# First layer of two small items with both halves of x in one matmul, and second-layer weights read as loaded

## The chip, the core and the metric

The kernel runs on one core of one Trainium2 chip. The metric is the time of one execution in microseconds (us), the median of several runs. The engines go by the names of the profile: PE is TensorE (with PEld for its weight loads), DVE is VectorE, ACT is ScalarE, POOL is GpSimd, SP is SyncE, whose queue issues most of the loads from memory.

## The reference

First a windowed attention over 8 sequences of 576 tokens and 8 heads; its output, 4608 tokens of 512 numbers, goes to a mixture of experts. Tokens with a positive skip score are sent to the best of 8 experts, a two-layer network, and its result, weighted with the gate, is added.

```python
skip_score = x @ w_skip
do_compute = skip_score > 0
xc = x[do_compute]
logits = xc @ w_gate
e_idx = np.argmax(logits, axis=1)
gate_w = softmax(logits)[np.arange(len(xc)), e_idx]
for e in range(8):
    mask = e_idx == e
    h = np.maximum(xc[mask] @ w1[e], 0.0)        # 512 -> 1024
    y[mask] = gate_w[mask, None] * (h @ w2[e])   # 1024 -> 512
out[do_compute] = xc + y
```

## The kernel before

The attention fills the first 162 us of the profiled execution; the change doesn't touch it. Towards its end the tokens are counted and listed for the experts, and the experts' work begins.

**Items and steps.** The experts are ranked by their number of tokens, and each rank has a fixed capacity. An item is a block of tokens of one expert: 256, 256, 144 (the rest of the second expert), 368, 336, 288, 256, 240, 160 and 112 (the rest of the first). Each item has four steps, one for each quarter (256 hidden units) of its expert. In step k the generator `expert_chunks` emits the first layer of step k (`up`) and the second layer of step k - 2 (`down`).

**Two parts of every operand.** Products are made in three matmuls: each operand is split into a rounded high part and a low rest, and `mm3` adds high by high, high by low and low by high in PSUM. For x this gives the tiles xh and xl, for the weights whi and wlo, for the hidden layer hh and hl.

**First layer.** For items of more than 128 tokens `up` makes two halves (f = 0, 1) of 128 hidden units each. In each it runs over four chunks c of 128 inputs, with three matmuls per chunk: the weights are the stationary operand, x of all n tokens the moving one, the sum stands in the PSUM tile p1 (tag "t", two buffers, in turn). Then ScalarE makes hh = relu(p1), rounded, and VectorE makes hl = max(p1, 0) - hh. Where the last 128-token tile of an item has 32 tokens or fewer (the items of 144, 288 and 160; the code calls them small), ScalarE also makes hp, a plain copy of relu(p1) for these last tokens.

**Second layer.** `down` multiplies tile by tile with `mm3`; for the last tile of a small item `down_small` multiplies hp with plain fp32 weights instead, four narrow matmuls side by side. These weights are loaded a second time for that purpose by `load_plain` into the tiles wr (256 KB a time, four buffers).

**Weights.** Each expert has eight pieces of 128 x 1024 numbers (512 KB): four of the first layer (w = 0) and four of the second (w = 1). SP's queue loads a piece into one of six raw tiles (`weight_dma`), ScalarE copies it rounded to whi (`weight_hi`), VectorE subtracts for wlo (`weight_lo`). whi and wlo stand in a ring of nine slots, each free again after the last use of its piece. `weights_to` is called before each chunk of the generator; it loads ahead by up to six pieces beyond the last one split and splits one more piece per chunk while the ring has room.

**x of the next item** is fetched by an indirect load (`gather_x`) and transposed on TensorE into the PSUM tile px (tag "g", one buffer); ScalarE copies xh and VectorE subtracts for xl (`split_x`). This happens within the steps of the item before, at the points (quarter, half) in `SPLITS`, after the `yield` of that half, so that the next weight split is emitted first.

**Order.** The order of the instructions on each engine is that of the program, with no planner: each engine takes its own in turn and waits at the first that isn't ready.

Of the kernel before, what the change touches and what calls it, by code (L numbers as in the profile page):

```python
# [8 lines left out]
F32 = mybir.dt.float32  # L9
# [4 lines left out]
ALU = mybir.AluOpType  # L14
# [51 lines left out]
OOB = 1 << 20  # L66
NWR = 4
XN = max(n for _, n, _ in ITEMS)
# [75 lines left out]
def window_attention_moe(ctx: ExitStack, tc, a, out):  # L144
# [667 lines left out]
    ring, used = [], {}  # L812
    raws = [early.tile([P, 1024], F32, name=f"raw{i}") for i in range(NRAW)]

    def ring_slots(pool, n):
# [12 lines left out]
    def weight_dma(n):  # L828
        e, qi, w = pieces[n]
        if e not in wrow:  # L830
            r = e % E
            ix = perm[0:1, r : r + 1] if r < 2 else tables["order"][0:1, r : r + 1]
            wrow[e] = nc.values_load(ix, engines=[SP], min_val=0, max_val=(E - 1) * NQ * P)
        nc.sync.dma_start(
            raws[n % NRAW], a["wq"][bass.ds(wrow[e] + qi * P, P), w * 1024 : w * 1024 + 1024]
        )
# [5 lines left out]
    def weight_hi(n):  # L842
        nc.scalar.copy(ring[n % RING][0], raws[n % NRAW])  # L843

    def weight_lo(n, by):
        hi, lo = ring[n % RING]
        by.tensor_tensor(lo, raws[n % NRAW], hi.bitcast(F32), op=ALU.subtract)  # L847

# [4 lines left out]
    def weights_to(n):  # L853
        n = min(n, len(pieces), ptr["free"] + len(ring))
        while ptr["split"] < n:
            while ptr["dma"] < min(len(pieces), ptr["split"] + NRAW):
                if not can_load(ptr["dma"]):
                    break
                weight_dma(ptr["dma"])
                ptr["dma"] += 1  # L860
            if ptr["dma"] == ptr["split"]:
                break
            weight_split(ptr["split"])
            ptr["split"] += 1
        while ptr["dma"] < min(len(pieces), ptr["split"] + NRAW) and can_load(ptr["dma"]):
            weight_dma(ptr["dma"])
            ptr["dma"] += 1
# [3 lines left out]
    def can_load(n):  # L871
        return pieces[n][0] % E < 2 or "order" in tables
# [42 lines left out]
    class Item:  # L915
        def __init__(self, n, e=None):
# [3 lines left out]
            self.small = self.nt > 1 and self.rows[-1] <= 32  # L920
            self.hh, self.hl, self.hp, self.wr = {}, {}, {}, {}

# [8 lines left out]

        def split(self, xh, xl, j, px=None):
            xh, xl = xh[:, :, : self.n], xl[:, :, : self.n]
            self.xc = [(xh[:, c], xl[:, c]) for c in range(NDC)]
            return split_x(self.xg[j], xh, xl, j, px)

        def split_both(self, xh, xl, pxs):
            self.xc = [(xh[c // 2][:, c % 2], xl[c // 2][:, c % 2]) for c in range(NDC)]
            split_both(self.xg, xh, xl, pxs)
# [4 lines left out]
    def up(it, qi, wh, wl):  # L944
# [6 lines left out]
        if nt > 1:  # L951
            for f in range(2):
                p1 = psum.tile([P, n], F32, name="p1", tag="t", bufs=2, padded_shape=[P, 512])
                for c in range(NDC):
                    w = slice(c * FQ + f * P, c * FQ + f * P + P)
                    mm3(p1, wh[:, w], wl[:, w], *it.xc[c], c == 0, c == NDC - 1)
                nc.scalar.activation(hh[:, f], p1, AF.Relu)  # L957
                if it.small:
# [5 lines left out]
        else:  # L964
# [11 lines left out]
            nc.vector.tensor_tensor(hl, pt[:, :, :n], hh.bitcast(F32), op=ALU.subtract)  # L976

    def load_plain(it, h):
        if h < 2 * NQ:
            it.wr[h] = wr = hpool["y"].tile([P, D], F32, name="wr", bufs=NWR)  # L980
            c = 1024 + h % 2 * D
            nc.sync.dma_start(wr, a["wq"][bass.ds(wrow[it.e] + h // 2 * P, P), c : c + D])

# [31 lines left out]
    def down_small(it, qi, y, m):  # L1015

        for f in range(2):
            h = 2 * qi + f
            for z in range(4):
                nc.tensor.matmul(  # L1020
                    y[32 * z : 32 * z + m, 0:P],
                    it.hp[qi][:, f, :m],
                    it.wr[h][:, z * P : (z + 1) * P],
                    start=h == 0,
                    stop=h == 2 * NQ - 1,
                    skip_group_check=True,
                )
            load_plain(it, h + NWR)

# [45 lines left out]
    def expert_chunks():  # L1075
        for k in range(len(steps) + 2):
            rising = ()
            if k < len(steps):
                i, qi = steps[k]
                if its[i].small and qi == 1:  # L1080
                    for h in range(NWR):
                        load_plain(its[i], h)
                rising = up(its[i], qi, *piece(k, 0))
                for f, c in enumerate(rising):
                    yield k, c
                    if its[i].nt == 1:
                        break
                    if i + 1 < len(its):
                        pts = ((3, 0), (3, 2)) if i + 1 == 2 else SPLITS[its[i + 1].nt]
                        if (qi, f) in pts:  # L1090
                            its[i + 1].split(*xhl[1 + i % 2], pts.index((qi, f)))()
            if k >= 2:
# [27 lines left out]
    with tc.manual_schedule():  # L1120
# [136 lines left out]
        tables["lists"] = mr.tile([P, E, LT], I32, name="les")  # L1257
        xhl += [tuple(mr.tile([P, NDC, XN], F32R, name=f"x{h}{s}") for h in "hl") for s in "12"]
        ring_slots(mr, RING - len(ring))
        xfree.extend(xgs[4:])  # L1260

# [204 lines left out]
```

## Time and profile before

| | us |
|---|---|
| median of 3 runs | 421.97 (420.9 to 422.24) |
| the profiled execution, its own time | 418.07 |
| its span, first to last instruction | 416.3 |
| TensorE busy | 398.2 (96% of the span) |
| VectorE busy | 291.6 (70%) |
| ScalarE busy | 219.4 (53%) |

The profile is of one execution. The 144-token item takes its steps from 210.8 us of the span on, the 160-token item from 372.3 us on. Matmuls are pipelined: a row's duration includes the way through the array, so what a matmul costs in a stream is read from the distance between starts. In the list of instructions in order of time, a bracket at the end of a line gives the idle time of the engine before it and what ended it.

### The profile page before, as it was taken

Reading aid. Unit: us, or ns where it says so; the run is one execution under the profiler, and the core shown is the slowest. Engines: PE = TensorE matmul, PEld = TensorE weight load, DVE = VectorE, ACT = ScalarE, POOL = GpSimd, SP = SyncE. Lnnn points to the kernel's source line nnn. Section 1 sums busy time; section 2 is a strip of 40 time slices with the busy share of each in tenths; the row PEclk is TensorE's granted clock in tenths of the full one; section 3 lists DMA queues with packets and bytes.
Section 4 is the critical chain, followed back from the end, with each engine's and each line's share of the span. In section 5 each row is a group of like instructions: output and inputs, shape, how many; then the busy total and the mean of one; then the engine's idle time right before and its main releaser. Section 6 shows DMA issues by size and latency. Waiting matters only on the chain.

```text
span 416.3 us, 11734 instructions
## 1 busy us (share of the span) xinstructions
PE 398.2 (96%) x4687; PEld 334.5 (80%) x4687; DVE 291.6 (70%) x515; ACT 219.4 (53%) x389; POOL 157.6 (38%) x296
## 2 busy tenths in 40 slices
PE   8699999999999889899999999999999999999994
PEld 3587887878778678779988898898888889988873
DVE  3387899899799797999436679555556485656661
ACT  2477868767767695436224436234426355444540
POOL 1431168666958878557103115013016030100110
PEclk9999999999999999899999999999999999999999
DMA  8999999999995695636928937545388866667810
GB/s 296 406 326 375 408 368 382 410 386 310 366 413 195 204 362 173 196 128 219 311 82 254 324 117 258 183 161 205 117 250 291 264 206 202 221 203 244 265 55 23
DMA packets 38554, 105.73 MB, mean 254 GB/s; under 512 B 4864, under 2 KB 6272, under 8 KB 38496
## 3 DMA queue, kind: packets, MB, share of 16 engines
q1 hardware_dynamic: 34016, 93.51, 65.3%
q0 software_dynamic: 3200, 9.58, 6.5%
q10 hardware_dynamic: 1280, 1.85, 1.2%
q8 instruction: 38, 0.62, 0.6%
q14 instruction: 20, 0.16, 0.1%
HBM read 90.86 MB, written 14.39 MB: 253 GB/s over the span
## 4 chain that ended last, share of the span: by engine, by line
PE 68%; DMA 10%; issue 7%; DVE 7%; POOL 4%; ACT 2%; POOLq 0%; ACTq 0%; DVEq 0%
PE av L387 8%; PE p L911 7%; PE p L912 7%; PE p L913 7%; PE pt L284 6%; PE ps L251 5%; DMA out<-yo,les 5%; PE yv L911 3%; PE yw L911 3%; PE yw L912 3%; PE yw L913 3%; PE yv L912 3%; PE yv L913 3%; DMA q<-qT 2%; PE ps L237 2%
## 5 line engine op out<-in xcount | busy, mean ns | idle before, releaser
L847 DVE TENSOR_TENSOR wlo<-raw,whi 128x1024 fp32r<-128x1024 f32 x70 | 85.6, 1233 | 17.5 <-ACT whi L843 17.5
L957 ACT ACTIVATE hh<-p 128x256 fp32r<-128x256 f32 (+6 forms) x72 | 27.7, 384 | 127.3 <-PE p L913 123.0
L911 PE MATMUL p<-xh,whi 128*128 128x256 f32 (+6 forms) x288 | 85.9, 298 | 0.2 <-DVE hl L960 0.2
L912 PE MATMUL p<-xl,whi 128*128 128x256 f32 (+6 forms) x288 | 84.3, 293 | 0.8 <-DVE xl L892 0.8
L913 PE MATMUL p<-xh,wlo 128*128 128x256 f32 (+6 forms) x288 | 84.4, 293 | 0.6 <-DVE wlo L847 0.6
L843 ACT CAST whi<-raw 128x1024 fp32r<-128x1024 f32 x72 | 74.3, 1046 | 0.0
L1003 POOL DMA_INDIRECT out<-yo,les x18 | 17.6, 976 | 147.3 <-DVE yo L994 137.6
L960 DVE SCALAR_TENSOR_TENSOR hl<-p,hh 128x256 fp32r<-128x256 f32 (+6 forms) x72 | 30.1, 419 | 61.2 <-ACT hh L957 35.5
L911 PEld LDWEIGHTS p<-xh,whi 128*128 128x128 f32 x288 | 55.2, 192 | 3.7 <-issue 1.7
L912 PEld LDWEIGHTS p<-xl,whi 128*128 128x128 f32 x288 | 55.3, 192 | 2.1 <-DVE xl L892 1.1
L913 PEld LDWEIGHTS p<-xh,wlo 128*128 128x128 f32 x288 | 55.4, 192 | 0.8 <-DVE wlo L847 0.8
L276 ACT ACTIVATE s<-s 128x1024 f32<-128x1024 f32 x36 | 38.1, 1058 | 30.9 <-DVE s L271 30.8
L270 DVE TENSOR_REDUCE mx<-ps 128x8 f32<-128x1024 f32 x36 | 43.6, 1210 | 6.1 <-PE ps L251 6.1
L271 DVE TENSOR_TENSOR s<-ps,mx 128x1024 f32<-128x1024 f32 x36 | 44.1, 1225 | 4.6
L387 PEld LDWEIGHTS av<-vm,ptm 128*64 128x64 f32 x992 | 35.2, 138 | 12.2 <-issue 5.5
L387 PE MATMUL av<-vm,ptm 128*64 128x74 f32 x992 | 40.4, 233 | 3.4 <-POOL vm L356 1.4
L285 ACT COPY ptm<-pt 128x512 f32<-128x512 f32 x72 | 38.3, 581 | 5.9 <-PE pt L284 5.8
L284 PE MATMUL pt<-ident,s 128*128 128x128 f32 x288 | 39.9, 283 | 0.0
L251 PE MATMUL ps<-k,q 64*64 64x128 f32 x1024 | 33.6, 270 | 2.5 <-DMA q<-qT 2.5
L251 PEld LDWEIGHTS ps<-k,q 64*64 64x64 f32 x1024 | 30.0, 133 | 5.3 <-issue 3.1
L284 PEld LDWEIGHTS pt<-ident,s 128*128 128x128 f32 x288 | 31.6, 143 | 2.5 <-issue 0.3
L356 POOL COPY vm<-vm 64x1184 f32<-64x1184 f32 x16 | 18.6, 1166 | 34.9 <-ACT vm L355 29.2
(225 smaller groups left out, 699.9 us busy)
## 6 DMA issues: line engine op xcount, KB each, us to landing
raw<-wq SPq DMA_DIRECT2D x72, 512.0 KB, 4.7
vm<-vp SPq DMA_DIRECT2D x15, 592.0 KB, 9.1
vT<-vT SPq DMA_DIRECT2D x16, 512.0 KB, 8.3
out<-x SPq DMA_DIRECT2D x32, 256.0 KB, 7.3
q<-qT SPq DMA_DIRECT2D x14, 512.0 KB, 9.1
wr<-wq SPq DMA_DIRECT2D x24, 256.0 KB, 5.5
k<-kT SPq DMA_DIRECT2D x7, 640.0 KB, 8.6
k<-kT SPq DMA_DIRECT2D x7, 512.0 KB, 8.7
```

Source lines behind the costliest of these rows:

```text
L251: nc.tensor.matmul(ps[64 * hf : 64 * hf + 64, r, p], q[h, p], k[h, :, p], start=False, stop=p == 3, skip_group_check=True,)
L270: nc.vector.tensor_reduce(mx, flat, axis=AX.X, op=ALU.max)
L271: pace[0] = nc.vector.tensor_tensor(s, flat, mx.unsqueeze(2).to_broadcast([P, 8, P]), op=ALU.subtract)
L276: nc.scalar.activation(s, s, AF.Exp, scale=0.125)
L284: nc.tensor.transpose(pt[:, p], s[:, 4 * r + p], ident)
L285: nc.scalar.copy(ptm[:, 4 * r : 4 * r + 4], pt)
L387: nc.tensor.matmul(av[64 * hf : 64 * hf + 64, h // 4, (h % 4) * VW : (h % 4 + 1) * VW], ptm[:, (h % 2) * 4 + h // 2, 64 * hf : 64 * hf + 6 ...
L843: nc.scalar.copy(ring[n % RING][0], raws[n % NRAW])
L847: by.tensor_tensor(lo, raws[n % NRAW], hi.bitcast(F32), op=ALU.subtract)
L911: nc.tensor.matmul(o, lh, rh, start=first, stop=False, skip_group_check=parts)
L912: nc.tensor.matmul(o, lh, rl, start=False, stop=False, skip_group_check=parts)
L913: nc.tensor.matmul(o, ll, rh, start=False, stop=last, skip_group_check=parts)
```

## The change

- Items of more than 128 and up to 160 tokens (those of 144 and 160) keep xh and xl of a chunk side by side in one tile. In the first layer one matmul with whi moves both (2n columns), and one with wlo adds its product to the second half. VectorE adds the two halves of p1 with a reduce into a tile in SBUF (`rest`; the tile is hs for f = 0 and the finished table `found` for f = 1), makes hh from it with a max, and then hl. hp is made by ScalarE from `rest`.
- `down_small` reads its weights from the raw tile of the piece. `load_plain` and wr are gone. The raw tiles are handed out from a list (`idle`): a tile goes back after wlo is made, or, for the second-layer pieces of the three experts that have a small tile, after `down_small`. Two more raw tiles are added once the attention's memory is free, eight in all.
- The split of the next item's x stands before the `yield` of its half instead of behind it, so ahead of the next weight split. One of the splits, the second of the 144-token item's x, stays where it was.

```diff
@@ weights
+    idle, raw_of = list(raws), {}
+    plain = {e for _, n, e in ITEMS if P < n and 0 < n % P <= 32}
+    held_raw = lambda n: pieces[n][2] == 1 and pieces[n][0] in plain
...
+        raw_of[n] = idle.pop(0)
         nc.sync.dma_start(
-            raws[n % NRAW], a["wq"][bass.ds(wrow[e] + qi * P, P), w * 1024 : w * 1024 + 1024]
+            raw_of[n], a["wq"][bass.ds(wrow[e] + qi * P, P), w * 1024 : w * 1024 + 1024]
         )
...
-        by.tensor_tensor(lo, raws[n % NRAW], hi.bitcast(F32), op=ALU.subtract)
+        by.tensor_tensor(lo, raw_of[n], hi.bitcast(F32), op=ALU.subtract)
+        if not held_raw(n):
+            idle.append(raw_of.pop(n))
...
-            while ptr["dma"] < min(len(pieces), ptr["split"] + NRAW):
+            while ptr["dma"] < len(pieces) and idle:
@@ Item.split
-        def split(self, xh, xl, j, px=None):
+        def split(self, xh, xl, pair, j, px=None):
             xh, xl = xh[:, :, : self.n], xl[:, :, : self.n]
+            self.pairs = [pair[:, c, :, : self.n] for c in range(NDC)] if P < self.n <= PAIRED else None
@@ up
-                p1 = psum.tile([P, n], F32, name="p1", tag="t", bufs=2, padded_shape=[P, 512])
+                p1 = psum.tile([P, 2 * n if it.pairs else n], F32, name="p1", tag="t", bufs=2, padded_shape=[P, 512])
                 for c in range(NDC):
                     w = slice(c * FQ + f * P, c * FQ + f * P + P)
-                    mm3(p1, wh[:, w], wl[:, w], *it.xc[c], c == 0, c == NDC - 1)
-                nc.scalar.activation(hh[:, f], p1, AF.Relu)
+                    if it.pairs:
+                        nc.tensor.matmul(
+                            p1, wh[:, w], it.pairs[c], start=c == 0, stop=False, skip_group_check=True
+                        )
+                        nc.tensor.matmul(
+                            p1[:, n:], wl[:, w], it.xc[c][0],
+                            start=False, stop=c == NDC - 1, skip_group_check=True,
+                        )
+                    else:
+                        mm3(p1, wh[:, w], wl[:, w], *it.xc[c], c == 0, c == NDC - 1)
+                if it.pairs:
+                    room = found.rearrange("p v e j -> p (v e j)") if f else pool.tile([P, FQ], F32, name="hs")
+                    rest = room[:, :n]
+                    nc.vector.tensor_reduce(rest, p1.rearrange("p (z n) -> p n z", z=2), axis=AX.X, op=ALU.add)
+                    p1 = rest
+                    nc.vector.tensor_scalar(hh[:, f], p1, 0.0, None, op0=ALU.max)
+                else:
+                    nc.scalar.activation(hh[:, f], p1, AF.Relu)
                 if it.small:
                     nc.scalar.activation(hp[:, f, : it.rows[-1]], p1[:, n - it.rows[-1] :], AF.Relu)
@@ down_small
+        n = when[it.e, qi, 1]
...
-                    it.wr[h][:, z * P : (z + 1) * P],
+                    raw_of[n][:, f * D + z * P : f * D + (z + 1) * P],
...
-            load_plain(it, h + NWR)
+        idle.append(raw_of.pop(n))
@@ expert_chunks
-                if its[i].small and qi == 1:
-                    for h in range(NWR):
-                        load_plain(its[i], h)
                 rising = up(its[i], qi, *piece(k, 0))
                 for f, c in enumerate(rising):
+                    if i + 1 < len(its) and its[i].nt > 1:
+                        pts = ((3, 0), (3, 2)) if i + 1 == 2 else SPLITS[its[i + 1].nt]
+                        if (qi, f) in pts:
+                            its[i + 1].split(*xhl[1 + i % 2], pts.index((qi, f)))()
                     yield k, c
                     if its[i].nt == 1:
                         break
-                    if i + 1 < len(its):
-                        pts = ((3, 0), (3, 2)) if i + 1 == 2 else SPLITS[its[i + 1].nt]
-                        if (qi, f) in pts:
-                            its[i + 1].split(*xhl[1 + i % 2], pts.index((qi, f)))()
@@ once the attention's memory is free
+        for s in "12":
+            pair = mr.tile([P, NDC, 2, XN], F32R, name=f"xp{s}")
+            xhl.append((pair[:, :, 0], pair[:, :, 1], pair))
...
+        idle.extend(mr.tile([P, 1024], F32, name=f"raw{NRAW + i}") for i in range(MORERAW))
```

## Rows read from the trace of the kernel before

**Rows 1.** Busy time by stage: stretch, length, busy us (and instructions) per engine, PEclk, DMA.

```profile
210.80:232.50 21.70, 21.70 (x178) 19.12 (x176) 11.88 (x19) 10.15 (x25) 4.99 (x5) 1.00 0.59 193
372.30:393.20 20.90, 20.90 (x169) 18.20 (x168) 12.66 (x20) 11.00 (x25) 1.94 (x2) 1.00 0.83 266
```

**Rows 2.** Waits of TensorE after 162 us: who waited for whom, us, times, longest.

```profile
PE pt L974 <- DVE hl L976: 0.2, 1, 0.2
```

**Rows 3.** TensorE in order of time: start us, duration us, line, out<-in, moving shape.

```profile
217.03 0.27 PE L912 MATMUL p<-xl,whi 128*128 128x144 f32 x1
...
218.81 0.28 PE L913 MATMUL p<-xh,wlo 128*128 128x144 f32 x1
...
297.08 0.30 PE L911 MATMUL p<-xh,whi 128*128 128x288 f32 x1
...
298.55 0.29 PE L913 MATMUL p<-xh,wlo 128*128 128x288 f32 x1
...
377.81 0.24 PE L911 MATMUL p<-xh,whi 128*128 128x160 f32 x1
377.88 0.28 PE L912 MATMUL p<-xl,whi 128*128 128x160 f32 x1
...
379.00 0.28 PE L913 MATMUL p<-xh,wlo 128*128 128x160 f32 x1
```

**Rows 4.** The weight loads of the same moment, in order of time.

```profile
377.81 0.19 PEld L912 LDWEIGHTS p<-xl,whi 128*128 128x128 f32 x1
377.92 0.19 PEld L913 LDWEIGHTS p<-xh,wlo 128*128 128x128 f32 x1
```

**Rows 5.** VectorE by line and shape: two reduces; xcount, busy us, mean ns, idle before.

```profile
L270 DVE TENSOR_REDUCE mx<-ps 128x8 f32<-128x1024 f32 x36 | 43.6, 1210 | 6.1 <-PE ps L251 6.1
...
L1336 DVE TENSOR_REDUCE val<-onh 128x44 f32<-128x352 f32 x1 | 0.5, 509 | 0.0
```

**Rows 6.** ScalarE, then VectorE, in the second step of the 160-token item.

```profile
379.31 0.30 ACT L957 ACTIVATE hh<-p 128x160 fp32r<-128x160 f32 x1 [2.79 <-PE p L913]
379.51 0.19 ACT L959 ACTIVATE hp<-p 128x32 f32<-128x32 f32 x1
379.59 1.05 ACT L843 CAST whi<-raw 128x1024 fp32r<-128x1024 f32 x1
...
380.67 1.23 DVE L847 TENSOR_TENSOR wlo<-raw,whi 128x1024 fp32r<-128x1024 f32 x1 [0.61 <-ACT whi L843]
381.81 0.32 DVE L960 SCALAR_TENSOR_TENSOR hl<-p,hh 128x160 fp32r<-128x160 f32 x1
...
383.18 1.40 DVE L994 SCALAR_TENSOR_TENSOR yo<-yv,got,xg 128x512 f32<-128x512 f32 x2
```

**Rows 7.** TensorE in order of time: first matmuls of steps of both items.

```profile
216.29 0.23 PE L911 MATMUL p<-xh,whi 128*128 128x144 f32 x1
...
222.16 0.23 PE L911 MATMUL p<-xh,whi 128*128 128x144 f32 x1
...
372.35 0.24 PE L911 MATMUL p<-xh,whi 128*128 128x160 f32 x1
...
383.25 0.24 PE L911 MATMUL p<-xh,whi 128*128 128x160 f32 x1
...
387.99 0.34 PE L911 MATMUL p<-xh,whi 128*128 128x160 f32 x1
...
393.22 0.37 PE L911 MATMUL p<-whi,xh 128*112 128x256 f32 x1
```

**Rows 8.** VectorE and TensorE around 187 us, in order of time.

```profile
183.42 3.17 DVE L847 TENSOR_TENSOR wlo<-raw,whi 128x1024 fp32r<-128x1024 f32 x2
...
187.24 0.39 PE L912 MATMUL p<-xl,whi 128*128 128x256 f32 x1 [0.75 <-DVE xl L892]
```

**Rows 9.** Loads by line: out<-in, queue, xcount, KB each, median us to landing.

```profile
raw<-wq SPq DMA_DIRECT2D x72, 512.0 KB, 4.7
...
wr<-wq SPq DMA_DIRECT2D x24, 256.0 KB, 5.5
```

More of the change, by code (lines that the diff above doesn't have):

```diff
@@ L66 @@
 OOB = 1 << 20
-NWR = 4
+PAIRED = 160
+MORERAW = 2
 XN = max(n for _, n, _ in ITEMS)
@@ L842, in weight_hi @@
     def weight_hi(n):
-        nc.scalar.copy(ring[n % RING][0], raws[n % NRAW])
+        nc.scalar.copy(ring[n % RING][0], raw_of[n])
     def weight_lo(n, by):
         hi, lo = ring[n % RING]
-        by.tensor_tensor(lo, raws[n % NRAW], hi.bitcast(F32), op=ALU.subtract)
+        by.tensor_tensor(lo, raw_of[n], hi.bitcast(F32), op=ALU.subtract)
+        if not held_raw(n):
+            idle.append(raw_of.pop(n))
     def weight_split(n):
@@ L864, in weights_to @@
             ptr["split"] += 1
-        while ptr["dma"] < min(len(pieces), ptr["split"] + NRAW) and can_load(ptr["dma"]):
+        while ptr["dma"] < len(pieces) and idle and can_load(ptr["dma"]):
             weight_dma(ptr["dma"])
@@ L920, in __init__ @@
             self.small = self.nt > 1 and self.rows[-1] <= 32
-            self.hh, self.hl, self.hp, self.wr = {}, {}, {}, {}
+            self.hh, self.hl, self.hp = {}, {}, {}
         def lists(self, idx, gate, r, j0=0):
@@ L937, in split_both @@
         def split_both(self, xh, xl, pxs):
+            self.pairs = None
             self.xc = [(xh[c // 2][:, c % 2], xl[c // 2][:, c % 2]) for c in range(NDC)]
@@ L976, in up @@
             nc.vector.tensor_tensor(hl, pt[:, :, :n], hh.bitcast(F32), op=ALU.subtract)
[L978 to L982, printed above, removed]
     def finish(y, xg, idx, gate, small):
@@ L1257, in window_attention_moe @@
         tables["lists"] = mr.tile([P, E, LT], I32, name="les")
-        xhl += [tuple(mr.tile([P, NDC, XN], F32R, name=f"x{h}{s}") for h in "hl") for s in "12"]
+        for s in "12":
+            pair = mr.tile([P, NDC, 2, XN], F32R, name=f"xp{s}")
+            xhl.append((pair[:, :, 0], pair[:, :, 1], pair))
         ring_slots(mr, RING - len(ring))
+        idle.extend(mr.tile([P, 1024], F32, name=f"raw{NRAW + i}") for i in range(MORERAW))
         xfree.extend(xgs[4:])
```

## Prediction

> **What bounds the kernel now.** I read the stages first: busy time per engine in the stretches of the two items that change. While the 144-token item runs (210.8 to 232.5 us) and while the 160-token item runs (372.3 to 393.2 us) TensorE is busy from end to end at full clock (2.4 GHz), VectorE for 11.9 of 21.7 us and 12.7 of 20.9 us, ScalarE for about half [rows 1]. A share can hide short waits, so the waits come next: the list of TensorE's waits after 162 us has six entries, none inside these items; the last and shortest is a pt that waits 0.2 us for VectorE's hl in the final item [rows 2], and one other matters here, an xl at 187 us (part 4). So TensorE's own order sets the end in both items, and VectorE has the room that the change will use. The question is what TensorE will wait for instead.
>
> **Part 1: three matmuls become two.** The starts of TensorE's matmuls tell what one costs, since its rows overlap. The 144-token item starts one every 0.111 us (217.03 to 218.81, 16 steps), the 160-token item too (377.88 to 379.00, 10 steps), with 11% more columns; at 288 columns it is 0.134 us (297.08 to 298.55, 11 steps) [rows 3]. So at 144 and 160 the step isn't the columns. The weight loads show what it is: they start 0.11 us apart as well (377.81, 377.92), and a matmul may start 0.07 us behind the start of its load (load 377.81, matmul 377.88) [rows 3, 4]. A 128x128 load of 4-byte weights costs 0.112 us and the short matmul hides under the next one. After the change a chunk has two loads. Load A at 0, long matmul A at 0.07, load B at 0.112, matmul B when A's columns are through (0.07 + 0.134 = 0.20 at 288 columns; 0.07 + 0.149 = 0.22 at 320, scaled by columns), next load A at 0.224. The pair costs two loads, 0.224 us instead of 0.336. The other end: if the next load can't run under the long matmul in this way, 0.134 + 0.112 = 0.246 and 0.149 + 0.112 = 0.261. I take 0.224, because the load at 377.81 starts as soon as the matmul before it starts [rows 3, 4]. Each item has 32 chunks (4 quarters x 2 halves x 4): 32 x 0.112 = 3.6 us saved in each, 0.9 in each of its four steps; at the other end 2.9 and 2.4.
>
> Here a page of the Trainium skill speaks against the change: "TensorE: Matmul & The Clock Gate", section "Back-to-back issue gap", gives an isolated matmul a warm gap of N/2.4 + 2.5 ns, by which three of 144 columns (an estimate of 187 ns) and one of 288 with one of 144 (185 ns) cost the same, so that an item would gain 0.1 us. The trace doesn't agree with that formula at 144 columns: 0.111 us, not 0.063.
>
> **Part 2: what VectorE gets.** Each half (16 in all) loses ScalarE's hh (0.30 us) and gains on VectorE a reduce from PSUM over 288 or 320 numbers and a max over half as many. No reduce over pairs is in the trace. The nearest rows: 352 numbers from SBUF 0.51 us, 1024 from PSUM 1.21 us [rows 5], 1.45 and 1.18 ns per number, so 320 cost 0.38 (1.18 ns each, nothing fixed) to 0.56 us (a tenth above the first scaled). I take 0.48, nearer to the row of like size. The max is no longer than hl's 0.32 us on as many numbers, and it runs while VectorE would wait anyway (next part).
>
> **Part 3: the new wait.** hp, the plain copy of the last 16 or 32 tokens, stays on ScalarE but now reads the result of the reduce. Queued behind it on ScalarE is the next whi; behind that whi, on VectorE, its wlo; behind that wlo the next half's reduce. Before, ScalarE waited only for TensorE and ran ahead: hp 379.51, whi 379.59, wlo 380.67, hl 381.81 [rows 6]. After, each half is one chain through both engines: reduce 0.48, hand-over 0.03, hp to whi 0.08, whi 1.05, hand-over 0.03, wlo up to the next VectorE operation 1.14: 2.81 us, so 5.6 us a step where TensorE wants 3.8 to 4.6. The max and hl (0.65) lie under the whi. And the reduce is what frees p1, of which there are two buffers: a half of the next step can't start before this step's same half is reduced.
>
> The 160-token item. Its steps start at 372.35, 377.81, 383.25, 387.99, and 393.22 ends the last [rows 3, 7]: 5.46, 5.44, 4.74, 5.23 us, after the saving 4.56, 4.54, 3.84, 4.33. A reduce can start 0.9 + 0.16 us into its step (hh came 0.16 us after the last of its matmuls' 1.34). Counted from 372.35, the reduces start at 1.06, 3.9, 6.7 and 9.5; two yo of the item before (1.3 us, 383.18 [rows 6]) push the next to 13.6, then 16.4, 19.2 and 22.6 (an xh of 0.5 stands before the last). TensorE would begin its fourth step at 12.9 and waits for the reduce of 13.6 to end at 14.1: 1.2 us; in that step's second half for the reduce of 16.4 to end at 16.9: 1.6 us; the next item's xl, behind the late reduce, is done at 21.0: 0.7 us more; the transposes of hs, behind the late whi, 0.2 us; and the pt that waits already [rows 2] 0.2 us more. That is 3.9 us of waits against 3.6 saved: 0.3 us later than before. With the reduce at 0.38 or 0.56 (seven halves long) it is 0.4 us sooner to 0.9 later.
>
> The 144-token item. Its four steps split one, two, one and two pieces, not always between the halves, so the chain closes in one place only. In its second step (216.29 to 222.16 [rows 7]) two wlo and two yo follow the second half and hold VectorE into the third; its xl is then done some 0.7 us after the next transposes want the same px (one buffer). Gain 3.6 - 0.7 = 2.9 us.
>
> **Part 4: x before the weights.** ScalarE's xh and VectorE's xl now go ahead of whi and wlo. At 187.24 TensorE had waited 0.75 us for an xl that ran behind two wlo (183.42, 3.17 us) [rows 8]. Now it is done near 184.1; the first of those wlo comes 0.7 us later, by half of the 3.17 near 185.7, still before its matmul at about 186.4. Gain up to 0.75 us; where VectorE is late again before 198 us some may go back, so I take 0.5, bounds 0 to 0.75. Elsewhere a wlo comes 0.7 us later, which the ring of nine hides, since eight pieces are split ahead; without that cover it would be 0.7 us for each of some 20 splits of x.
>
> **Part 5: plain weights.** 24 loads of 256 KB go [rows 9]; nothing on TensorE waited for them, so nothing is gained on the path. The raw tiles of the three experts now stay until the small matmuls have read them. Followed through the piece list, the loads issued ahead of the split are eight instead of six where nothing is held, four at the worst. On SP's queue later raw loads stand behind one that waits for a release; the tightest (piece 70 of 72) waits for the wlo near 19.4 after 372.35, lands 4.7 us later (median [rows 9]) at 24.1 and is split at 25.4. So it costs nothing; were a load 2 us late, the split would be, two steps ahead of its use.
>
> **Sum.** -2.9 + 0.3 - 0.5 = -3.1 us. The profiled execution took 418.07 us, with a span of 416.3: 415.0 after. The median of the runs, 421.97, lies 3.9 us above that execution; the same 3.1 us off it: 418.9.
>
> **Rivals.**
> 1. Both savings stay: -3.6 - 3.6 - 0.7 = -7.9, 414.1 us. VectorE would have to finish a half within TensorE's 1.9 to 2.3 us. For it: by busy time alone VectorE would need only a little more than TensorE, and the item has but four steps. Against: the order of hp, whi, wlo. Chance 0.15.
> 2. Slower: a reduce over pairs has one output for every two inputs, and pays for outputs too: 0.96 us instead of 0.48. A half is then 3.3 us, the 160-token item ends 7 x 0.48 = 3.4 us later still, the 144-token item loses 1.0 more: -1.9 - 0.5 + 3.7 = +1.3, 423.3 us. It decides from a reduce of about 0.8 us on. Against: 352 numbers into 44 outputs cost nothing visible over 1024 into 8 [rows 5]. Chance 0.13.
> 3. A matmul costs its columns, so that the pair takes what the three took, and TensorE gains nothing: part 4 alone is left, -0.5, 421.5 us. For it: above 256 columns the steps do grow with columns; against: the equal steps at 144 and 160 [rows 3]. Chance 0.06.
>
> The forecast has 0.66. Inside it the terms spread from -4.5 (short reduce, no wait for px, all of part 4) to -1.1 (pairs at 0.246, long reduce, nothing from part 4): 417.5 to 420.9. The range reaches from inside rival 1's neighbourhood to rival 3 and leaves out rival 2: 414.9 to 421.9. A change of 0.3% (1.3 us) is about what can be told from none. Faster by more: rival 1 and 0.52 of the forecast's 0.66, 0.67. Within: 0.18. Slower by more: rival 2 and 0.02 of unlooked-for stalls, 0.15.
>
> **What would show it.** Right: pairs of starts every 0.224 us and weight loads 0.112 apart; the 144-token item near 18.8 us instead of 21.7; whi starting 0.6 us behind each reduce's start; TensorE waiting for the reduce in the fourth step of the 160-token item; no wait at 187. Wrong: no TensorE wait in that item (rival 1), a reduce above 0.8 us (rival 2), steps of pairs at 0.33 (rival 3), or a whi that waits for its load (part 5).

## The result, and the profile after

The changed kernel takes 417.52 us (median; 415.9 to 418.89), beside 421.66 us for the kernel before in the same comparison: ratio 0.990 (95% interval 0.988 to 0.993), 4.1 us less. In two later comparisons (numbers 1 and 9 below; the kernel before took 417.79 and 417.74 us there) the ratio was 0.9947 (0.9918 to 0.9976) and 0.9950 (0.9927 to 0.9974), 2.1 to 2.2 us less. The forecast, 3.1 us, lies between.

The profiled executions begin the experts' first matmul between 161.0 and 166.7 us of their spans, the kernel before alone at 162.1 and at 165.3, though the change doesn't touch the attention that runs until then. So traces are compared below by stages, from one start in TensorE's timeline to another; ratios only between kernels that ran on the same chip.

Page of the changed kernel: busy time of each engine, the load queue, and the traffic of the whole execution.

```profile
PE 392.6 (95%) x4623; PEld 327.6 (79%) x4623; DVE 301.7 (73%) x547; ACT 216.7 (52%) x373; POOL 159.6 (38%) x296
...
q1 hardware_dynamic: 30560, 87.22, 60.1%
```

TensorE lost 5.6 us of busy time and 64 matmuls, VectorE gained 10.1 us. The load queue moved 6.3 MB less than the 93.51 of before: the 24 second loads of plain weights.

Changed kernel, busy time by stage (columns as in [rows 1]): the 144-token item, then the 160-token item.

```profile
210.77:230.28 19.51, 19.04 (x146) 16.24 (x144) 14.24 (x30) 6.83 (x15) 5.63 (x5) 1.00 0.35 110
370.60:391.56 20.96, 18.81 (x137) 15.74 (x135) 15.57 (x30) 7.71 (x15) 1.94 (x2) 1.00 0.31 100
```

Against [rows 1] the 144-token item is 2.2 us shorter. The 160-token item is as long as before, 21 us, but TensorE is now busy for 18.8 of them only. Where before no wait lay inside either item [rows 2], TensorE now waits twice for a reduce inside the 160-token item, and for x at the start of the item behind each of the two.

Changed kernel, waits of TensorE after 162 us: who waited for whom, us, times, longest.

```profile
PE p L966 <- DVE found L978: 1.2, 1, 1.2
PE p L918 <- ACT xp L896: 0.7, 2, 0.4
PE p L966 <- DVE hs L978: 0.6, 1, 0.6
...
PE pt L999 <- DVE hl L1001: 0.4, 1, 0.4
PE p L919 <- DVE xp L899: 0.2, 1, 0.2
...
PE p L920 <- DVE xp L899: 0.2, 1, 0.2
```

L966 is the first matmul of a pair and L978 the reduce: TensorE waits for the reduce to free p1. The waits in L918 to L920 are for the two parts of the next item's x; pt are the transposes of the hidden layer in the last item.

The stages of all kernels, in us, from starts in the timelines of TensorE. "First" runs from the first `up` matmul to the 144-token item's first, "144" and "between" to the first matmuls of the next item and of the 160-token item, "160" from there to the third pt of the last item, so that it also holds what the 160-token item pushes into the item behind it. Each block is one comparison, on one chip.

| kernel | first | 144 | between | 160 |
|---|---|---|---|---|
| before, as profiled ahead | 48.76 | 21.68 | 139.85 | 31.50 |
| changed | 46.71 | 19.51 | 140.32 | 32.32 |
| | | | | |
| changed, again | 48.65 | 19.04 | 139.73 | 32.78 |
| hp on GpSimd | 47.92 | 19.47 | 140.64 | 30.32 |
| only the 144-token item paired | 48.58 | 19.04 | 139.73 | 31.52 |
| no item paired | 48.57 | 21.69 | 139.73 | 31.52 |
| | | | | |
| before, again | 46.79 | 22.69 | 141.05 | 31.49 |
| hp on VectorE | 47.56 | 20.04 | 140.58 | 29.06 |
| x behind | 46.59 | 20.19 | 140.34 | 35.21 |
| reduce twice | 46.74 | 22.53 | 139.80 | 36.54 |
| | | | | |
| changed, third time | 48.31 | 19.05 | 139.73 | 32.32 |
| hp on VectorE, again | 48.64 | 18.75 | 139.73 | 29.06 |
| hp on VectorE, x behind | 48.95 | 18.74 | 140.02 | 29.30 |

So the 144-token item gives 2.6 us (2.2 in the first execution, where TensorE then waited 0.4 and 0.2 us for x) and the 160-token item takes 0.8 to 1.3 us back. "First" has two patterns, whatever the kernel: near 48.6 where TensorE waits 1.3 us for VectorE at about 171 us and the granted clock is at 0.50 for some microseconds behind that wait, near 46.7 where neither comes within the stage. Between them lie 48.31 (the wait, and no fall of the clock), 47.92 (both) and 47.56 (neither). In the third block TensorE waited for the x of the item behind the 144-token item in the kernel before too (0.94 and 0.93 us), so that stage is compared within the block.

### The profile page after: what moved, and what is told of

It reads as the page before. It is cut to its first block, busy times and chain, and to the rows that moved or that the text cites. A ratio compares the mean times of both kernels' runs of the same rounds, so it can differ in the third digit from the quotient of the medians.

```text
span 415.4 us, 11519 instructions
## 1 busy us (share of the span) xinstructions
PE 392.6 (95%) x4623; PEld 327.6 (79%) x4623; DVE 301.7 (73%) x547; ACT 216.7 (52%) x373; POOL 159.6 (38%) x296
## 4 chain that ended last, share of the span: by engine, by line
PE 64%; issue 13%; DMA 10%; DVE 4%; POOL 4%; ACT 3%; POOLq 0%; ACTq 0%; SPq 0%; another core or an unknown queue 0%; DVEq 0%
PE av L388 8%; PE pt L285 7%; PE p L918 6%; PE ps L252 5%; PE p L919 5%; PE p L920 5%; DMA out<-yo,les 5%; PE yv L918 3%; PE yv L919 3%; PE yv L920 3%; PE ps L238 2%; PE pw L336 2%; PE yw L919 2%; PE yw L918 2%; PE yw L920 2%
## 5 line engine op out<-in xcount | busy, mean ns | idle before, releaser
L982 ACT ACTIVATE hh<-p 128x256 fp32r<-128x256 f32 (+4 forms) x56 | 22.9, 410 | 98.3 <-PE p L920 84.5
L918 PE MATMUL p<-xp,whi 128*128 128x256 f32 (+4 forms) x192 | 58.2, 303 | 0.4 <-ACT xp L896 0.4
L919 PE MATMUL p<-xp,whi 128*128 128x256 f32 (+4 forms) x192 | 57.1, 297 | 0.2 <-DVE xp L899 0.2
L920 PE MATMUL p<-xp,wlo 128*128 128x256 f32 (+4 forms) x192 | 56.8, 296 | 0.0
L985 DVE SCALAR_TENSOR_TENSOR hl<-p,hh 128x256 fp32r<-128x256 f32 (+4 forms) x56 | 25.2, 451 | 43.5 <-ACT hh L982 28.0
L918 PEld LDWEIGHTS p<-xp,whi 128*128 128x128 f32 x192 | 36.2, 188 | 3.0 <-ACT xp L896 0.7
L919 PEld LDWEIGHTS p<-xp,whi 128*128 128x128 f32 x192 | 36.2, 188 | 1.2 <-DVE xp L899 0.5
L920 PEld LDWEIGHTS p<-xp,wlo 128*128 128x128 f32 x192 | 36.1, 188 | 0.0
```

Source lines behind the costliest of these rows:

```text
L918: nc.tensor.matmul(o, lh, rh, start=first, stop=False, skip_group_check=parts)
L919: nc.tensor.matmul(o, lh, rl, start=False, stop=False, skip_group_check=parts)
L920: nc.tensor.matmul(o, ll, rh, start=False, stop=last, skip_group_check=parts)
```

## Experiments

**Theory.** The pair saves TensorE's time in both items. In the 160-token item the saving is lost, because hp on ScalarE waits for the reduce, and whi, wlo and the next reduce are queued behind it. **Rivals:** VectorE simply has too much work; or the second item's pairing still gains something and the loss comes from elsewhere; or parts 4 and 5 of the prediction (x ahead of the weights, plain weights from the raw tiles) bring the gain.

**1. The changed kernel again**, as the comparison for the next three. No edit.

> The changed kernel unchanged, timed beside the others of this set. Theory A (the 144-token item gains, the 160-token item gives its saving back to the chain reduce, hp, whi, wlo): about 0.990 of before, 417.5 us where before has 421.7, and again a wait for the reduce of 0.6 and 1.2 us in the fourth step of the 160-token item. Theory B (most of the gain comes from elsewhere, since the two profiled executions differ by 0.9 us only): the same time, but the stage of the 144-token item not shorter by 2 us.

415.59 us, ratio 0.9947 (0.9918 to 0.9976), where about 0.990 was expected. The two waits for the reduce are there again, 0.63 and 1.21 us. What is new is TensorE's clock behind the second. Busy time by stretch, this run:

```profile
386.80:387.90 1.10, 0.56 (x6) 0.34 (x4) 1.01 (x1) 0.05 (x1) 0.32 (x1) 1.00 0.78 287
387.90:388.60 0.70, 0.03 (x1) 0.03 (x1) 0.67 (x3) 0.05 (x1) 0.00 (x0) 1.00 0.68 225
388.60:389.60 1.00, 1.00 (x5) 1.00 (x6) 0.52 (x2) 1.00 (x2) 0.00 (x0) 0.58 0.02 8
389.60:390.60 1.00, 1.00 (x6) 1.00 (x6) 0.86 (x1) 0.11 (x1) 0.00 (x0) 0.50 0.00 0
390.60:391.60 1.00, 1.00 (x4) 0.81 (x4) 0.97 (x3) 0.14 (x2) 0.00 (x0) 0.50 0.00 0
391.60:392.60 1.00, 1.00 (x4) 0.62 (x3) 0.83 (x3) 1.00 (x3) 0.00 (x0) 0.72 0.35 90
```

The column behind the five engines is the granted clock. TensorE had been nearly idle from 387.4 to 388.57; then it works at 0.50 (1.2 GHz) until about 392. This stage took 32.78 us with only the two waits in it, where the first execution took 32.32 with five.

**2. hp on GpSimd**, in the paired items.

```diff
-                if it.small:
+                if it.small and it.pairs:
+                    nc.gpsimd.tensor_scalar(
+                        hp[:, f, : it.rows[-1]], p1[:, n - it.rows[-1] :], 0.0, None, op0=ALU.max
+                    )
+                elif it.small:
                     nc.scalar.activation(hp[:, f, : it.rows[-1]], p1[:, n - it.rows[-1] :], AF.Relu)
```

> hp of the two paired items is made by GpSimd instead of ScalarE, so that whi no longer waits for the reduce. Theory A: the chain falls apart, reduces in the 160-token item come 2.2 us apart at the closest where they came 2.87, TensorE does not wait for them in the fourth step, xl is in time; the item ends 2.5 to 3.3 us sooner than in the changed kernel (its saving at 0.26 per pair is 2.4, and it lost 0.8 in the profile): 414.5 us. Rival (VectorE itself is too full, by its sum of busy time): within 1 us of the changed kernel.

414.89 us, ratio 0.9924 (0.9898 to 0.9950): not to be told from the changed kernel's by time, but the 160 stage is 2.5 us shorter (30.32) and has no wait for a reduce in the fourth step. A new wait takes its place. GpSimd, then an instruction that only GpSimd's queue shows (name, count, shortest, median and longest in ns, start), then VectorE, in this run:

```profile
381.89 0.95 POOL L1026 DMA_INDIRECT out<-yo,les  x1 [0.30 <-DVE hh L980]
386.93 0.29 POOL L984 TENSOR_SCALAR hp<-hs 128x32 f32<-128x32 f32 x1 [4.09 <-ACT whi L848]
```

```profile
L1124 POOLq DRAIN  x1: 5804/5804/5804, 381.0 to 381.0; - x1
```

```profile
387.25 0.49 DVE L978 TENSOR_REDUCE hs<-p 128x160 f32<-128x320 f32 x1 [1.93 <-POOL hp L984]
```

hp runs at 386.93, 5.6 us after the reduce of 380.83 was through. What stands ahead of it in GpSimd's queue is the `drain` that both kernels put behind the scatters of the 240-token item: it lasts 5.8 us from 380.95, to 386.76, and ScalarE's whi in the bracket of hp merely ended near that moment. The next reduce into that buffer waits 1.93 us for it. TensorE then waits for the reduce and for x at the start of the next item (0.35 and 0.62 us). In the 144-token item the waits are 0.65 and 0.65 us; there is no drain there, but hp stands behind five indirect transfers on GpSimd (two scatters, three fetches of x, from 221.10 to 227.45). So with hp out of ScalarE's queue the two waits of the fourth step are gone, as the chain wants it, and this place for hp has delays of its own.

**3. Only the 144-token item paired.**

```diff
-PAIRED = 160
+PAIRED = 144
```

> Only the 144-token item is paired; the 160-token item has three matmuls and hh on ScalarE as before. Theory A: the same as the changed kernel or up to 0.8 us faster, 416.7 to 417.5, since the 160-token item gained nothing. Rival (both items gain 2.4 us or more): 420 us, 2.4 us slower than the changed kernel.

415.66 us, ratio 0.9936 (0.9911 to 0.9962), as the changed kernel's 0.9947. The 160 stage is that of before (31.52). So pairing the 160-token item gains nothing as the change makes it: its stage is 0.8 to 1.3 us longer with it, and the medians can't be told apart.

**4. No item paired** (parts 4 and 5 alone).

```diff
-PAIRED = 160
+PAIRED = 128
```

> No item is paired; the plain weights from the raw tiles and x before the weights stay. Theory A: 2 to 2.3 us slower than the changed kernel (the 144-token item's 2.2 less 0.2, and the 160-token item's 0.8 the other way: 1.2 to 2.3 in all), about 419. Theory B: within 1 us of the changed kernel, so 417.5, and the gain lies in parts 4 and 5. If these parts give nothing: 421.7.

418.19 us, ratio 0.9992 (0.9970 to 1.0013). Alone, x first and the plain weights from raw change nothing that can be told; the 144 stage is 21.69 again. Experiment 3 differs from this run by the pairing of the 144-token item alone, and the two intervals don't touch: 2.5 us, beside 2.7 in the stage.

**5. hp on VectorE**, right behind hh, in the paired items.

```diff
-                if it.small:
+                if it.small and it.pairs:
+                    nc.vector.tensor_scalar(
+                        hp[:, f, : it.rows[-1]], p1[:, n - it.rows[-1] :], 0.0, None, op0=ALU.max
+                    )
+                elif it.small:
                     nc.scalar.activation(hp[:, f, : it.rows[-1]], p1[:, n - it.rows[-1] :], AF.Relu)
```

> The changed kernel with hp of the items of 144 and 160 tokens made by VectorE (a max over the last 16 or 32 columns, right behind hh) instead of ScalarE; GpSimd's queue of gathers is not in its way as it was when hp stood on GpSimd. Theory A (the wait of ScalarE's hp for the reduce, with whi, wlo and the next reduce queued behind it, is what the 160-token item loses): whi no longer follows the reduce, a half costs VectorE about 0.52 + 0.27 + 0.25 + 0.15 (estimate for hp, from the 0.24 us of the max over 160) + 1.14 = 2.3 us, 4.7 a step against TensorE's 4.8, so the two waits of 0.6 and 1.2 us in the fourth step go or shrink below 0.6 in sum; the 144-token item keeps its gain; the stretch from the 160-token item's first matmul to the third pt is 30.0 to 31.0 us (32.3 and 32.8 with hp on ScalarE, 31.5 before), and the ratio to the kernel before is 0.989 to 0.992. Theory B (VectorE's work itself is too long, whoever makes hp): waits for the reduce of 1 us and more remain, the stretch stays above 32 us, ratio as the changed kernel's, 0.994 to 0.996.

415.99 us, ratio 0.9875 (0.9846 to 0.9903). The 160 stage is 29.06 us, shorter than the 30.0 expected. The rows are shown at experiment 10.

**6. x behind**: the split of x back behind the `yield`, the rest as changed.

```diff
                 for f, c in enumerate(rising):
-                    if i + 1 < len(its) and its[i].nt > 1:
-                        pts = ((3, 0), (3, 2)) if i + 1 == 2 else SPLITS[its[i + 1].nt]
-                        if (qi, f) in pts:
-                            its[i + 1].split(*xhl[1 + i % 2], pts.index((qi, f)))()
                     yield k, c
                     if its[i].nt == 1:
                         break
+                    if i + 1 < len(its):
+                        pts = ((3, 0), (3, 2)) if i + 1 == 2 else SPLITS[its[i + 1].nt]
+                        if (qi, f) in pts:
+                            its[i + 1].split(*xhl[1 + i % 2], pts.index((qi, f)))()
```

> The changed kernel with the split of the next item's x put back behind the yield, as in the kernel before (part 4 undone). Theory A (part 4 exchanges one wait for another): TensorE waits about 0.75 us for an xl near 187 us of the span again and no longer 0.4 us or more for GpSimd's one-hot product; from the first up matmul to the 144-token item the time is 48.4 to 49.0 us; the time is within 0.2% of the changed kernel's, ratio to the kernel before 0.993 to 0.997. Theory B (part 4 brings 0.5 us or more that the wait for GpSimd doesn't take back): this stretch is 0.5 us longer than the 48.6 of the kernels with x first, and the ratio 0.1 to 0.2% above the changed kernel's. Theory C (x first costs, by pushing weight splits): ratio 0.2% or more below the changed kernel's, and in the 144- and 160-token items the waits for the reduce shrink.

420.79 us, ratio 0.9990 (0.9961 to 1.0018): 4.8 us above experiment 5 on the same chip (which differs from it in two edits), and no gain left over the kernel before. None of the three theories had that. ScalarE in this run, then TensorE:

```profile
393.20 0.23 ACT L984 ACTIVATE hp<-hs 128x32 f32<-128x32 f32 x1 [1.76 <-DVE hs L978]
393.34 1.03 ACT L848 CAST whi<-raw 128x1024 fp32r<-128x1024 f32 x1
394.27 0.52 ACT L896 CAST xp<-px 128x448 fp32r<-128x448 f32 x1
```

```profile
394.85 0.37 PE L918 MATMUL p<-whi,xp 128*112 128x256 f32 x1 [1.27 <-ACT xp L896]
...
396.21 0.37 PE L920 MATMUL p<-whi,xp 128*112 128x256 f32 x1 [0.88 <-DVE xp L899]
```

The copy of x for the last item stands behind hp and whi, which hang on the late reduce; TensorE waits 1.27 and 0.88 us for its two parts, where the changed kernel waits 0.33 and 0.17. Behind that the clock falls here too:

```profile
396.30:397.30 1.00, 1.00 (x6) 1.00 (x7) 0.82 (x3) 0.71 (x2) 0.00 (x0) 0.65 0.74 291
397.30:398.30 1.00, 1.00 (x6) 1.00 (x6) 0.51 (x1) 0.46 (x1) 0.00 (x0) 0.50 0.15 45
398.30:400.00 1.70, 1.70 (x6) 1.31 (x5) 0.91 (x2) 1.54 (x3) 0.00 (x0) 0.50 0.00 0
```

The 160 stage is 35.21 us, 2.4 to 2.9 above that of the changed kernel. Beside the changed kernel's third execution, where the clock stays up, the matmul behind the second wait starts 1.7 us later in the stage (23.28 and 21.62 us from its start); the rest of the 2.9 comes at the low clock. The wait for xl near 187 us that theory A wanted didn't come back: the execution was of the other pattern of "first", with 1.66 us for GpSimd's one-hot product (an operand of the listing of tokens) there, as in the kernel before of this block.

**7. Reduce twice.**

```diff
                     nc.vector.tensor_reduce(rest, p1.rearrange("p (z n) -> p n z", z=2), axis=AX.X, op=ALU.add)
+                    nc.vector.tensor_reduce(rest, p1.rearrange("p (z n) -> p n z", z=2), axis=AX.X, op=ALU.add)
```

> The changed kernel with the reduce of each half issued twice, one after the other, with the same operands: 0.48 us more in the chain of each of the 16 halves. Theory A (in the 160-token item the chain reduce, hp, whi, wlo, next reduce sets the pace, in the 144-token item TensorE does): reduces of the 160-token item 3.3 us apart instead of 2.86; TensorE's two waits in the fourth step grow from 0.6 and 1.2 us by about four and one more halves (to 2.5 and 1.7 us), the stretch from the item's first matmul to the third pt from 32.3 or 32.8 us by 2.4 to 3.4; the 144-token item grows by 0 to 1.0 us; ratio to the kernel before 1.000 to 1.005. Theory B (slack on VectorE hides it): both items as in the changed kernel, within 0.3 us, ratio 0.993 to 0.996.

424.42 us, ratio 1.0081 (1.0050 to 1.0111), more than theory A said. Reduces of the 160-token item in this run, the first of each of two following halves:

```profile
378.64 0.49 DVE L978 TENSOR_REDUCE found<-p 128x160 f32<-128x320 f32 x1
...
382.03 0.49 DVE L978 TENSOR_REDUCE hs<-p 128x160 f32<-128x320 f32 x1
```

3.39 us apart where the changed kernel has 2.86: the chain sets the pace. The 160 stage grew by 3.8 to 4.2 us, not 2.4 to 3.4: TensorE waits 1.69 and 1.70 us for reduces, at 386.57 in the third step already, and the clock falls behind both (0.50 from 388.0 to 391.4 and from 394.8 to 398.2 us). The 144 stage grew by 2.3 us against "x behind" in the same block, where 0 to 1.0 was expected. TensorE waits 0.37 us and, at the transposes of x in the fourth step (229.33), 1.71 us, where "x behind" waits 1.06 for x at the end of the stage; and behind the longer wait the clock falls in this item too, from 230.9 us to the end of the stage. One stretch of it:

```profile
231.90:232.90 1.00, 1.00 (x4) 0.63 (x2) 0.80 (x2) 1.00 (x3) 0.00 (x0) 0.50 0.71 164
```

In both items theory B falls. That 0.5 us more in another link of the chain would do the same wasn't tried.

**8. The kernel before again**, for a second profile by stage. No edit.

> The kernel before, unchanged, for a second profile of it by stage. Both theories: 144-token item 21.7 us, from the 160-token item's first matmul to the third pt 31.5 us, the wait of about 0.75 us for an xl near 187 us; if one of these differs by more than 0.3 us, that term can't be read from single profiles.

421.59 us in its one run. The 160 stage is 31.49 us, as in the first profile. The 144 stage is 22.69, with the waits for x of this block, and there is no wait for an xl near 187 us, but 1.66 us for GpSimd a little ahead of it. So those two terms can't be read from one profile.

**9. The changed kernel a third time**, beside the next two. No edit.

> The changed kernel as it is, beside the next two. By theory A of the runs before (the chain over ScalarE costs the 160-token item two waits of 0.6 and 1.2 us, and in some executions a fall of TensorE's clock behind them; the 144-token item gains 2.5): from the 160-token item's first matmul to the third pt 32.3 to 32.8 us, ratio to the kernel before 0.990 to 0.996. If these waits belong to one chip or one execution only, the stretch is 29.5 to 31.5 us here.

415.60 us, ratio 0.9950 (0.9927 to 0.9974); 32.32 us with waits of 0.63, 1.20, 0.32, 0.17 and 0.35 us, as in the first execution, and the clock stays at 1.00.

**10. hp on VectorE again**, the edit of experiment 5.

> The changed kernel with hp on VectorE in the items of 144 and 160 tokens, on the same chip as the changed kernel itself. Theory A: this stretch is 29.1 us again with no wait for a reduce, 3.2 to 3.7 us shorter than the changed kernel's; the medians of the two differ by 2 to 4 us, ratio to the kernel before 0.985 to 0.990. Theory B (the ratio of 0.9875 was the chip's, not the edit's): the two medians lie within 1 us.

413.13 us, ratio 0.9873 (0.9846 to 0.9900), 2.5 us under the changed kernel on the same chip, with the interval wholly below that one's. Theory A holds. Busy time of its two items, then VectorE and ScalarE in the second step of the 160-token item:

```profile
212.39:231.14 18.75, 18.75 (x146) 16.20 (x144) 15.60 (x38) 7.50 (x9) 5.05 (x5) 1.00 0.36 112
370.87:389.29 18.42, 18.42 (x138) 15.71 (x136) 16.59 (x38) 7.68 (x8) 1.95 (x2) 1.00 0.40 130
```

```profile
377.59 0.17 DVE L984 TENSOR_SCALAR hp<-hs 128x32 f32<-128x32 f32 x1
377.71 0.33 DVE L989 SCALAR_TENSOR_TENSOR hl<-hs,hh 128x160 fp32r<-128x160 f32 x1
377.95 1.22 DVE L852 TENSOR_TENSOR wlo<-raw,whi 128x1024 fp32r<-128x1024 f32 x1
379.09 0.48 DVE L978 TENSOR_REDUCE found<-p 128x160 f32<-128x320 f32 x1
```

```profile
375.92 1.05 ACT L848 CAST whi<-raw 128x1024 fp32r<-128x1024 f32 x1 [1.84 <-PE yv L920]
```

TensorE is busy from end to end in both items. VectorE does one us more work in the 160-token item than in the changed kernel, 16.6 of 18.4 us, and yet holds nobody up: whi now stands ahead of the reduce (375.92; the reduce before it in the program starts at 376.90), so that wlo follows hl at once. That answers the rival of too much work.

**11. hp on VectorE, x behind**: both edits.

> hp on VectorE, and the split of the next item's x put back behind the yield. Theory A (x first pays only where the chain over ScalarE makes whi and wlo late, since the split of x then stands behind them): with the chain cut, putting x back costs under 0.5 us in the 160-token item (stretch to the third pt 29.0 to 29.6 us) and the ratio is within 0.15% of the run with x first. Theory B (x first is worth 2 us or more whatever the chain): TensorE waits 1 us or more for the copies of x at the 112-token item, stretch above 30.5 us, ratio 0.4% or more above.

413.79 us, ratio 0.9895 (0.9868 to 0.9921); 160 stage 29.30 us. With the chain cut, x behind costs 0.24 us there and 0.3 us in "first", where TensorE waits 0.84 us for an xl at 188.4 in place of 0.37 us for GpSimd. Theory A holds for the stage; the ratios differ by 0.2%, where 0.15% was the limit expected, and their intervals overlap.

## Why the prediction was right, point by point

The mechanism came as forecast: the pairs save TensorE's time, and in the 160-token item the chain of reduce, hp, whi and wlo takes the saving back. That the total came near the forecast is in part luck: the terms as measured add up to -2.0 us, where the forecast had -3.1 and the first comparison gave -4.1.

**Part 1, mis-sized.** The prediction took 0.224 us for a pair and kept 0.246 and 0.261 as the other end. Changed kernel, TensorE in the 160-token item, then its weight loads of the same moment:

```profile
371.00 0.24 PE L969 MATMUL p<-xp,wlo 128*128 128x160 f32 x1
371.07 0.35 PE L966 MATMUL p<-xp,whi 128*128 128x320 f32 x1
371.26 0.24 PE L969 MATMUL p<-xp,wlo 128*128 128x160 f32 x1
```

```profile
371.00 0.19 PEld L966 LDWEIGHTS p<-xp,whi 128*128 128x128 f32 x1
371.11 0.19 PEld L969 LDWEIGHTS p<-xp,wlo 128*128 128x128 f32 x1
371.26 0.19 PEld L966 LDWEIGHTS p<-xp,whi 128*128 128x128 f32 x1
```

A pair takes 0.259 us; in the 144-token item pairs start at 210.97, 211.22, 211.46 and 211.70, 0.245 apart. That is the other end. The step that failed is the choice between the ends: the load at 377.81 that starts together with the matmul before it [rows 4] was read as a load that can follow at 0.112 us whatever runs. The rows after show that the load of the next whi starts only with the short matmul (371.26 and 371.26), so only one load runs ahead, and the long matmul's columns and one load add up. The section "LDWEIGHTS (loading the stationary operand)" of the Trainium skill's page "TensorE: Matmul & The Clock Gate" gives P/1.2 ns for a load, an estimate of 107 ns for 128 columns; the 0.11 us between the loads of 371.00 and 371.11 agree. An item saves 32 x (0.336 - 0.245) = 2.9 and 32 x (0.336 - 0.259) = 2.5 us instead of 3.6. Experiment 10 measures just that, with no new wait: 18.75 for 21.68 us, and 29.06 for 31.50.

**Part 2, right.** 0.48 us a reduce at 320 numbers (0.45 at 288), and 0.24 for the max. Rival 2 wanted 0.8.

**Part 3, 160-token item: mechanism right, a little too short.** VectorE, then ScalarE, in the second step of the item, changed kernel:

```profile
374.66 0.48 DVE L978 TENSOR_REDUCE found<-p 128x160 f32<-128x320 f32 x1
...
376.38 1.23 DVE L852 TENSOR_TENSOR wlo<-raw,whi 128x1024 fp32r<-128x1024 f32 x1 [0.60 <-ACT whi L848]
377.52 0.48 DVE L978 TENSOR_REDUCE hs<-p 128x160 f32<-128x320 f32 x1
```

```profile
375.18 0.23 ACT L984 ACTIVATE hp<-found 128x32 f32<-128x32 f32 x1 [1.69 <-DVE found L978]
375.31 1.04 ACT L848 CAST whi<-raw 128x1024 fp32r<-128x1024 f32 x1
```

Reduce at 374.66, hp at 375.18, whi at 375.31 (0.65 behind the reduce's start; 0.6 was said), wlo at 376.38, the next reduce at 377.52: 2.86 us for 2.81. Counted from the item's start the eight reduces began at 1.19, 4.06, 6.92, 9.78, 13.96, 16.82, 19.68 and 23.03, where the prediction had 1.06, 3.9, 6.7, 9.5, 13.6, 16.4, 19.2 and 22.6. The waits came in the fourth step: 0.62 for 1.2 and 1.21 for 1.6 us, smaller because TensorE itself was slower by its pairs and came to its fourth step at 13.9, not 12.9; then 0.33 and 0.17 for the next x (0.7 said), and 0.35 at the pt, 0.2 above before, as said. The rows of the new waits sum to 2.5 us, the stage lost 29.06 to 32.32, 3.3 us. About 0.7 lies outside the rows. Laid beside experiment 10 matmul by matmul, the first execution falls back by 0.69 us at the wait of 0.62, by 1.44 at that of 1.21, and by 0.4 at each of those of 0.33 and 0.17: a restart costs more than its row says, since an idle time is counted from the modelled end of the matmul before, and in a stream matmuls overlap. Net +0.8 us where +0.3 was forecast. The prediction didn't ask what the clock does behind such a wait; in one of three executions of the changed kernel it cost some 1.6 us more (worked out from the matmul starts of 388.57 to 391.9, which are about twice as far apart as in the others), and the waits for x then vanished.

**Part 3, 144-token item: near, by two errors.** 2.9 us was 3.6 less 0.7 for px. The pairs gave 2.9, and the wait for px was 0.3 (in the fourth step, not the third; in the third run of the changed kernel its transposes start at 226.12, 0.31 behind a matmul at 225.81, where they follow after 0.07 in experiment 10): 2.6 in two executions, 2.2 in the first.

**Part 4, wrong place.** The 0.75 us for an xl at 187 us goes, but in its place TensorE waits 0.4 to 0.5 us (1.76 in other executions) for GpSimd's one-hot product just ahead of it. Within the executions near 48.6, "first" fell from 48.76 and 48.95 (x behind) to 48.57 to 48.65 (x first): 0.1 to 0.4 us (hp on GpSimd, at 47.92, had neither wait). In the other pattern there is nothing to gain: 46.79 and 46.59 behind, 46.71 and 46.74 first. Where x first does count is the place that the prediction passed by with "an xh of 0.5 stands before the last": it keeps the copies of x from being caught behind hp and whi in the chain of part 3. Without it the stage is 2.4 to 2.9 us longer; of the 2.9 some 1.7 come by the waits and the rest by the clock's fall behind them (experiment 6). When the chain is cut, x first is worth 0.24 us there (experiment 11).

**Part 5, right.** No whi waited for its load after 190 us in the changed kernel, and no pairing means no difference (experiment 4).

**Sum.** By measured terms of the changed kernel: -2.6 + 0.8 - 0.2 = -2.0 us, or -2.6 + 1.3 - 0.1 = -1.4 when the clock falls. That fits the 2.1 and 2.2 us of the later comparisons better than the 4.1 of the first; what the first gave beyond it stays open. Its two profiled executions don't show it: from the 144-token item to the end the changed one is 0.9 us shorter (-2.2, +0.5 between, +0.8). Held against the second profile of the kernel before (experiment 8), from a comparison whose median for that kernel, 421.32, is close to the 421.66 of the first, it is 3.1 us shorter: there TensorE waited 0.94 and 0.93 us for x behind the 144-token item, and in the changed kernel 0.39 and 0.23. Whether the executions of the first comparison had these waits, no profile shows. Three sums of the prediction don't come out, without effect on its range: a tenth above the first reduce scaled to 320 numbers is 0.51 us, not 0.56; the terms named for -4.5 add up to -4.75, and those for -1.1 to about -1.3.

**Rivals.** Rival 1 (both savings stay) fell as the kernel is written, and would have come true, at smaller size, with hp on VectorE: -2.9 - 2.4 - 0.1 = -5.4 by stages, 4.6 us less by the medians (experiment 10). Its condition, VectorE done with a half within TensorE's time, is met there (halves 2.2 to 2.7 us apart, 3.5 where the two yo stand between). Rival 3 fell: the equal steps at 144 and 160 columns [rows 3] were the load, not the columns.

## What to carry to other kernels

When work moves to another engine, follow the in-order queue behind the smallest instruction that now depends on it: a copy of 0.2 us that waits holds every piece of work behind it, and moving that copy to the engine that makes its input was worth more here than the added work cost. Matmuls merged to save a weight load can save less than the load: here a long one and a short one cost the long one's columns plus a load, 0.245 and 0.259 us for 0.336. An edit that gains nothing alone may be what keeps another from losing, so undo parts in both settings.

## What the runs showed of the hardware

- TensorE's load of the next weights ran only one matmul ahead: with moving sizes 320 and 160 in turn the loads start 0.11 and 0.15 us apart, not evenly.
- A wait of 1.2 us of TensorE in the middle of full work was in one of three executions of the changed kernel followed by some 3.4 us at 1.2 GHz; with waits of 1.27 and 0.88 us, or 1.7 us, it followed too. What decides it, these runs don't settle.
- GpSimd took 0.29 us for a max over 32 numbers and VectorE 0.17, but GpSimd's came up to 5.6 us late: in the 160-token item behind a drain of 5.8 us in its queue, in the 144-token item behind five indirect transfers of about 1 us each.
